# Attention with top-32 masking, then a gated MLP, on one core: the second exponential ahead of the score copies, normalisation in the same turn, and w3's products issued from a list

## The chip, the cores and the metric

The kernel runs on one core of a Trainium2 chip. The metric is the device time of one execution in microseconds (us), lower being better. The five engines are named as in the profile: PE (TensorE matmul, with PEld for its weight loads), DVE (VectorE), ACT (ScalarE), POOL (GpSimd) and SP (SyncE, which issues all DMAs here).

## What is computed

Batch 8, 8 heads, 576 positions, head dimension 64; all float32. Cut to what matters, the reference is:

```python
scores = np.matmul(q, k.transpose(0, 1, 3, 2)) / np.sqrt(D)
kth = np.partition(scores, -32, axis=-1)[..., -32:-31]
scores = np.where(scores >= kth, scores, -1e9)
attn = np.exp(scores - scores.max(-1, keepdims=True))
attn = attn / (attn.sum(-1, keepdims=True) + 1e-9)
x = np.matmul(attn, v)                # heads joined: 4608 tokens x 512
return ((x @ w1) * (x @ w2)) @ w3 @ w_out     # 512 -> 1024 -> 1024 -> 512
```

The kernel multiplies w3 with w_out once, at the start, and uses the product (wf) for all tokens.

## The kernel before, in words

**Slots and turns.** The attention is cut into 144 slots, 18 for each batch entry. A slot is 128 query rows of two heads, or, for every fifth of a head pair (t == 4), the last 64 rows of two head pairs. The main loop of `attn_moe` runs one turn per value of `p`, and works on four slots in it: scores of slot i = p+1 (PE), the search for the 32 largest of slot p (DVE), mask and exponentials of slot j = p-1 (ACT and POOL), and transposes, values and output of slot m = p-2 (PE, ACT, DVE). An engine runs its instructions in the order in which the code issues them (`InOrder`).

**Names.** `st` are the two PSUM tiles of a slot's scores, `s` their copy in SBUF. `w` is the search's working copy, `top` the 32 maxima, `edge` what bias the mask and the exponential need from them. `pab` holds a slot's weights: the mask (ACT, then a POOL subtraction `pab<-s,pab`), the exponential (ACT, with the row sums `sums`), and the normalisation (POOL, `pab<-pab,sums`), for which `enlarge` adds 1e-9 to the sums on POOL and `invert` takes their reciprocal on DVE. `tp` and `ro` are the transposes, `pts` and `pr` their copies (ACT), and `ro` then takes the values' product too; `xf` is the attention's output, as a high half (ACT) and a low half (DVE).

**PSUM.** Transposes and scores share one pool of two buffers (`ps_a`): in a turn tp, st and st take them in rotation, so that the next turn's tp waits until the first st has been copied by ACT and read by DVE's first two search instructions. `ro` has one buffer, which is free again when DVE has read it for the low half of xf. The third pool (three buffers) serves the MLP, the weights' decoding and w3's products.

**The MLP.** Every 18 turns a batch entry's MLP is queued as a list of 576 matmuls. `fill(SHARE[k])` issues 11, 11 and 10 of them at three places of each turn. Their results are taken by closures (`take_a`: ACT copy `asb`; `take_b`: DVE product `whole`, ACT cast `g`, POOL remainder `g`; `take_o`: ACT copy `osb` and a DMA), which `evict()` issues at the head of the next fill. Two thirds of the matmuls are ab (x times w1 and w2), one third eo (times wf).

**The start.** Weights arrive as 64-bit values and are decoded on the way (ACT twice, DVE twice, POOL once for each of 40 pieces: 8 of w_out, 16 of w3, 8 of w1, 8 of w2), in steps that `warm()` advances at five places of a turn; every second call starts another piece. A w3 piece issues its four products with w_out (`pf`) as soon as it is decoded, wherever that falls in the turn; when a tile pf is complete, ACT and DVE split it into wf.

Of the kernel before, what the change touches and what calls it, by code (L numbers as in the profile page):

```python
# [14 lines left out]
ALU = mybir.AluOpType  # L15
# [42 lines left out]
def attn_moe(ctx: ExitStack, tc: tile.TileContext, q, k, v, w1, w2, w3, w_out, out, flag, general):  # L58
# [12 lines left out]
    pe, act, dve, pool, sp = nc.tensor, nc.scalar, nc.vector, nc.gpsimd, nc.sync  # L71
# [26 lines left out]
    if not general:  # L98
        pe, act, dve, pool, sp = (InOrder(tc, e) for e in (pe, act, dve, pool, sp))
# [7 lines left out]
    def decode(z, dst=None):  # L107

        t = ps_m.tile([128, 512], F32, tag="mm", name="t")
        y = x_p.tile([128, 4 * HS], F32, tag="x", name="y")
        high = z[:, 1:1024:2]
        low = z[:, :1024].bitcast(U16)[:, 1:2048:4]
        u, r = y[:, :512].bitcast(I32), y[:, 512:1024].bitcast(I32)
        sign = z[:, :512].bitcast(I32)
        act.activation(t, high, AF.Copy, scale=2.0**-112)
        act.activation(r, low, AF.Copy, scale=2.0**-13)  # L120
        yield
        ti = t.bitcast(I32)
        dve.tensor_scalar(sign, ti, -(2**31), None, op0=ALU.bitwise_and)
        dve.scalar_tensor_tensor(u, ti, 3, sign, op0=ALU.logical_shift_left, op1=ALU.bitwise_or)
        yield
        dst = y[:, :512] if dst is None else dst
        pool.tensor_tensor(dst.bitcast(I32), u, r, op=ALU.add)
        yield
        yield
        return dst  # L130
# [10 lines left out]
    def load_wout(c, z):  # L141
        yield from decode(z, wo[:, c * 512 : (c + 1) * 512])

    fold = {}

    def load_w3(c, z):
        f, i = c // 2, c % 2
        y = yield from decode(z)
        if i == 0:
            fold[f] = ps_m.tile([128, 512], F32, tag="mm", name=f"pf{f}")  # L150
        for j in range(4 * i, 4 * i + 4):
            pe.matmul(
                fold[f], y[:, (j % 4) * 128 : (j % 4 + 1) * 128], wo[:, j * DM : (j + 1) * DM],
                start=(j == 0), stop=(j == NFC - 1),
            )
        if i == 1:
            cut = slice(f * DM, (f + 1) * DM)
            yield
            act.copy(wf[0][:, cut], fold[f])
            yield  # L160
            dve.tensor_tensor(wf[1][:, cut], fold[f], wf[0][:, cut].bitcast(F32), op=ALU.subtract)
# [37 lines left out]
    def new_s():  # L199
        return att_p.tile([128, 2, S], F32, tag="s", name="s", bufs=3)  # L200
# [5 lines left out]
    def behind(ins, first, why):  # L206
        tc.add_manual_dep(
            ins.ins, first.ins.name, mybir.DependencyInfo(mybir.DependencyClass.Sync, mybir.DependencyReason.DATA),
            reason=why,
        )  # L210

    def top32_steps(s, st, taken, slot):

        w = att_p.tile([128, 2, S], F32, tag="w", name="w", bufs=1)
        top = tops[slot % len(tops)]  # L220
        one, two, three = slice(0, NG), slice(NG, 2 * NG), slice(2 * NG, S)
        in_two, in_three = st[0][:, :, NG : 2 * NG], st[1][:, :, :NG]
        dve.tensor_tensor(w[:, :, three], s[:, :, one], in_two, op=ALU.max)
        yield dve.tensor_tensor(w[:, :, two], s[:, :, one], in_two, op=ALU.min)
        ins = dve.tensor_tensor(w[:, :, one], w[:, :, three], in_three, op=ALU.max)
        behind(ins, taken, "one engine at a time reads a bank of the scores")
        dve.tensor_tensor(w[:, :, three], w[:, :, three], in_three, op=ALU.min)
        yield
        for i in range(4):
            cut = slice(i * 8, (i + 1) * 8)  # L230
            for a in range(2):
                dve.max(top[:, a, cut], w[:, a, one] if i < 3 else w[:, a, :])
            if i < 3:
                for a in range(2):
                    dve.match_replace(w[:, a, one], top[:, a, cut], w[:, a, one], NEG)
                yield
# [7 lines left out]
    def compare(slot):  # L244
        top = tops[slot % len(tops)]
        pool.tensor_tensor(over[:, 2 * slot : 2 * slot + 2], top[:, :, 31], top[:, :, 23], op=ALU.subtract)
# [23 lines left out]
    def exps(edge, pab, sums, a):  # L270
        p = pab[:, a, :]
        act.activation(p, p, AF.Exp, bias=edge[:, a, 0:1], scale=SCALE, accum_out=sums[:, a : a + 1])

    def enlarge(sums):
        pool.tensor_scalar(sums, sums, 1e-9, None, op0=ALU.add)

    def invert(sums):
        dve.reciprocal(sums, sums)

    def normalise(pab, sums):  # L280
        for a in range(2):
            pool.tensor_scalar(pab[:, a, :], pab[:, a, :], sums[:, a : a + 1], 1.0, op0=ALU.mult, op1=ALU.mult)
# [40 lines left out]
    def take_high(to, ov):  # L323
        for x, cols, n in to:
            act.copy(x[:, 0, cols], ov[:, n])

    def take_low(to, ov):
        for x, cols, n in to:
            dve.tensor_tensor(x[:, 1, cols], ov[:, n], x[:, 0, cols].bitcast(F32), op=ALU.subtract)
# [69 lines left out]
    if general:  # L399
# [3 lines left out]
        with tc.For_i(0, B, 1) as b:  # L403
            seen = small.tile([1, 1], I32, tag="seen", name="seen", bufs=1)
            nc.sync.dma_start(seen, flag[ds(b + 1, 1), :])
            with tc.If(nc.values_load(seen, min_val=0, max_val=1) > 0):
                kv, xs = {}, {}
                for hps, t in SLOTS:
# [3 lines left out]
                    s, st = new_s(), scores([kv[hp] for hp in hps], t)  # L412
# [20 lines left out]
    kv, ss, sts, edges, pabs, xts, lows = {}, {}, {}, {}, {}, {}, {}  # L433
# [4 lines left out]
    def evict():  # L438
        while put_off:
            put_off.pop(0)()  # L440

    def fill(n):
        evict()
        while queue and n:
            if next(queue[0], "end") == "end":
                queue.pop(0)
            else:
                n -= 1
# [4 lines left out]
    def fetch_pair(u):  # L453
        if u < B * NHP:
            kv[u] = load_pair(u // NHP, u % NHP)

    waiting = list(startup)
    fetched, going, turns = [], [], []

    def prefetch(n):  # L460
        while waiting and len(fetched) < n:
            src, step = waiting.pop(0)
            fetched.append((fetch(src), step))

    def warm():

        if p < 0:
            return
        turns.append(p)
        if fetched and len(turns) % 2:  # L470
            z, step = fetched.pop(0)
            going.append(step(z))
        going[:] = [unit for unit in going if next(unit, "end") != "end"]
        prefetch(3)
# [4 lines left out]
    n_slots = len(slots)  # L479
    for p in range(-1, n_slots + 3):  # L480
        i, j, m = p + 1, p - 1, p - 2
        if i < n_slots and slots[i][1] == 3:
            fetch_pair(slots[i][0][0] + 2)
        finder = top32_steps(ss[p], *sts.pop(p), p) if 0 <= p < n_slots else iter(())
        next(finder, None)
        if 0 <= m < n_slots:
            enlarge(pabs[m][1])
            invert(pabs[m][1])
        if 0 <= j < n_slots:
            edges[j] = edges_of(j)  # L490
        if 0 <= m < n_slots:
            normalise(*pabs[m])
        next(finder, None)
        if m - 1 in lows:
            take_low(*lows.pop(m - 1))
            if m % NS == 0:
                b = m // NS - 1
                queue.append(moe_steps(b, [xts.pop(b * NHP + hp) for hp in range(NHP)], put_off.append))
        warm()
        if 0 <= j < n_slots:  # L500
            pabs[j] = new_weights()
            for a in range(2):
                mask(ss[j], edges[j], pabs[j][0], a)
            compare(j)
        fill(SHARE[0])
        next(finder, None)
        if 0 <= m < n_slots:
            tp, ro = turn(pabs[m][0])
            pts, pr = take_turned(tp, ro)
        warm()  # L510
        if 0 <= j < n_slots:
            exps(edges[j], *pabs[j], 0)
        fill(SHARE[1])
        next(finder, None)
        warm()
        if i < n_slots:
            st = scores(pairs_of(i), slots[i][1])
            ss[i] = new_s()
            take_scores(ss[i], st, 0)
        if 0 <= j < n_slots:  # L520
            exps(edges[j], *pabs[j], 1)
        if i < n_slots:
            sts[i] = st, take_scores(ss[i], st, 1)
        if 0 <= m < n_slots:
            us, t = slots[m]
            for u in us:
                if u not in xts:
                    xts[u] = new_x()
            ov = values([kv[u][2] for u in us], t, pts, pr, ro)
            lows[m] = places([xts[u] for u in us], t), ov  # L530
            take_high(*lows[m])
        next(finder, None)
        warm()
        fill(SHARE[2])
        for _ in finder:
            pass
        if 0 <= m < n_slots:
            del ss[m], pabs[m], edges[m]
        warm()
# [61 lines left out]
```

## Time and profile before

| | |
|---|---|
| median of 3 runs | 1324.32 us (1323.19 to 1325.38) |
| the profiled execution | 1324.6 us, span from its first to its last instruction 1322.8 us |
| busy: PE, DVE | 1225.7 us (93%), 1144.5 us (87%) |
| busy: ACT, POOL | 949.1 us (72%), 863.2 us (65%) |
| mean granted TensorE clock | 0.977 of full speed |

Shares over the whole span mix three stages: the start up to some 230 us, in which the weights are decoded beside the first 18 slots; the steady part, in which each turn carries its 32 MLP matmuls; and the last 93 us, in which only the last entry's MLP is left. So busy time is read by stage below. PE's matmuls are pipelined, so that a row's length is more than what it adds; what a group of matmuls costs is read from one start to the next.

### The profile page before, as it was taken

What the parts mean: (1) busy time and instruction counts of PE and PEld (TensorE: products, weight loads), DVE (VectorE), ACT (ScalarE), POOL (GpSimd) and SP (SyncE); (2) the same over time, 40 slices, a digit from 0 to 9 for tenths busy, and PEclk for the clock granted to TensorE, in tenths of its full rate; (3) what the DMA queues carried; (4) which work ended last, traced back from release to release, by engine and by line L of the source; (5) the groups of instructions that cost most, each with busy time, mean ns of one, the idle gap of its engine ahead of it and who ended that gap; (6) DMA issues with size and microseconds to landing.
All of it is one profiled execution on the core that took longest, in us unless ns stands there. A gap on an engine that the chain in (4) does not pass through costs nothing.

```text
span 1322.8 us, 30010 instructions
## 1 busy us (share of the span) xinstructions
PE 1225.7 (93%) x10513; PEld 1045.4 (79%) x10513; DVE 1144.5 (87%) x3980; ACT 949.1 (72%) x2025; POOL 863.2 (65%) x1201
## 2 busy tenths in 40 slices
PE   3688846999999999999999999999999999999996
PEld 1444424888888889888888888888988888888996
DVE  7989889999999999999999999999999999999100
ACT  5776687777777787777777777777777777777311
POOL 4767697776767676766667676767677676667210
PEclk9899877999999999999999999999999999999998
DMA  6343320001020201110010101010111001000000
GB/s 232 115 139 112 126 94 23 28 22 59 17 64 12 68 13 49 31 50 20 27 53 21 59 17 63 13 50 30 49 31 48 22 21 59 17 15 2 19 19 21
DMA packets 28981, 63.89 MB, mean 48 GB/s; under 512 B 3220, under 2 KB 11412, under 8 KB 28820
## 3 DMA queue, kind: packets, MB, share of 16 engines
q1 hardware_dynamic: 28820, 61.88, 14.4%
q8 instruction: 85, 1.39, 0.5%
q14 instruction: 76, 0.62, 0.2%
HBM read 52.43 MB, written 9.44 MB: 47 GB/s over the span
## 4 chain that ended last, share of the span: by engine, by line
PE 75%; POOL 10%; ACT 7%; issue 4%; DVE 3%; DMA 0%; SPq 0%; POOLq 0%; ACTq 0%; DVEq 0%
PE ab L49 26%; PE eo L49 16%; PE st L49 11%; PE ro L49 11%; PE tp L49 9%; POOL pab L49 5%; PE pf L49 3%; ACT pab L49 2%; ACT s L49 2%; POOL g L49 2%; DVE w L49 1%; POOL y L49 1%; DVE top L49 1%; ACT g L49 1%; ACT xf L49 1%
## 5 line engine op out<-in xcount | busy, mean ns | idle before, releaser
L49 DVE MAX8 top<-w 128x8 f32<-128x192 f32 (+1 forms) x1152 | 469.1, 451 | 0.0
L49 PE MATMUL ab<-xf,wh 128*128 128x288 f32 x2048 | 430.6, 300 | 0.0
L49 POOL TENSOR_TENSOR pab<-s,pab 128x576 f32<-128x576 f32 x288 | 404.6, 1429 | 4.7 <-ACT pab L49 4.7
L49 PEld LDWEIGHTS ab<-xf,wh 128*128 128x128 f32 x2048 | 331.3, 189 | 8.3 <-issue 7.4
L49 PE MATMUL ab<-xf,wl 128*128 128x288 f32 x1024 | 307.4, 300 | 0.0
L49 DVE MATCH_REPLACE8 w<-top,w 128x192 f32<-128x192 f32 x864 | 291.2, 347 | 0.0
L49 POOL TENSOR_SCALAR pab<-pab,sums 128x576 f32<-128x576 f32 x288 | 212.5, 753 | 78.4 <-DVE sums L49 57.9
L49 ACT COPY pts<-tp 128x1024 f32<-128x1024 f32 x144 | 146.2, 1015 | 152.7 <-PE tp L49 151.0
L49 ACT ACTIVATE pab<-s,edge 128x576 f32<-128x576 f32 x288 | 209.6, 782 | 54.6 <-POOL edge L49 52.4
L49 PE MATMUL eo<-g,wf 128*128 128x288 f32 x1536 | 228.4, 300 | 0.0
L49 ACT ACTIVATE pab<-pab,edge 128x576 f32<-128x576 f32 x288 | 225.2, 782 | 1.6 <-POOL pab L49 1.3
L49 PE MATMUL tp<-ident,pab 128*128 128x128 f32 x1152 | 166.1, 284 | 64.8 <-POOL pab L49 53.6
L49 ACT COPY s<-st 128x768 f32<-128x768 f32 (+1 forms) x288 | 181.9, 632 | 48.2 <-PE st L49 39.8
L49 PEld LDWEIGHTS eo<-g,wf 128*128 128x128 f32 x1536 | 208.1, 188 | 7.2 <-issue 7.2
L49 PEld LDWEIGHTS tp<-ident,pab 128*128 128x128 f32 x1152 | 134.6, 144 | 88.6 <-POOL pab L49 87.2
L49 PE MATMUL st<-kt,qt 64*128 64x192 f32 (+3 forms) x1280 | 188.8, 445 | 16.0 <-ACT pab L49 7.4
L49 PEld LDWEIGHTS ab<-xf,wl 128*128 128x128 f32 x1024 | 193.6, 189 | 4.8 <-issue 4.8
L49 POOL TENSOR_TENSOR g<-whole,g 128x288 fp32r<-128x288 f32 x128 | 103.0, 805 | 139.7 <-ACT g L49 139.7
L49 DVE TENSOR_TENSOR w<-s,st 128x384 f32<-128x384 f32 x288 | 146.7, 551 | 29.4 <-ACT s L49 18.3
L49 PEld LDWEIGHTS st<-kt,qt 64*128 64x128 f32 (+1 forms) x1280 | 100.2, 182 | 88.9 <-issue 34.8
L49 DVE TENSOR_TENSOR w<-w,st 128x384 f32<-128x384 f32 x288 | 157.7, 548 | 5.0
L49 PE MATMUL ro<-pts,vt 128*64 128x128 f32 (+1 forms) x2560 | 161.5, 269 | 0.0
(46 smaller groups left out, 1128.5 us busy)
## 6 DMA issues: line engine op xcount, KB each, us to landing
z<-in_w SPq DMA_DIRECT2D x32, 512.0 KB, 3.6
vt<-in_v SPq DMA_DIRECT2D x32, 352.0 KB, 3.5
kt<-in_k SPq DMA_DIRECT2D x32, 320.0 KB, 3.3
qt<-in_q SPq DMA_DIRECT2D x32, 288.0 KB, 2.9
out_t<-osb SPq DMA_DIRECT2D x64, 144.0 KB, 1.7
z<-in_wo SPq DMA_DIRECT2D x8, 512.0 KB, 5.0
flag<-missed SPq DMA_DIRECT2D x1, 0.0 KB
seen<-flag SPq DMA_DIRECT2D x1, 0.0 KB
```

The source lines that it names most:

```text
L49: ins = fn(*args, **kw)
```

## The change

In a turn, the first four search instructions now stand together; the second exponential follows the first, ahead of both score copies (before: copy, second exponential, copy). `enlarge`, `invert` and `normalise` work on slot j, behind its exponentials, in place of slot m at the head of the next turn: `enlarge` behind the cast of xf, the reciprocal on DVE behind the third search round and ahead of the last maxima, the normalisation on POOL behind it. w3's products go to a list, from which a turn takes up to 3 behind the masks, 1 behind the exponentials (between transposes and scores on PE) and 4 behind the values; a piece waits until its last product has been issued, and at most four pieces are under way.

```diff
+    fold, heavy = {}, []
+    def weigh(n):
+        while heavy and n:
+            heavy.pop(0)()
+            n -= 1
...
-        for j in range(4 * i, 4 * i + 4):
+        def product(j):
             pe.matmul(
...
+        heavy.extend((lambda j=j: product(j)) for j in range(4 * i, 4 * i + 4))
+        last = heavy[-1]
...
+        while last in heavy:
+            yield
...
-        yield dve.tensor_tensor(w[:, :, two], s[:, :, one], in_two, op=ALU.min)
+        dve.tensor_tensor(w[:, :, two], s[:, :, one], in_two, op=ALU.min)
...
-        if fetched and len(turns) % 2:
+        if fetched and len(turns) % 2 and len(going) < 4:
...
-        next(finder, None)
-        if 0 <= m < n_slots:
-            enlarge(pabs[m][1])
-            invert(pabs[m][1])
...
-        if 0 <= m < n_slots:
-            normalise(*pabs[m])
...
+        weigh(3)
         fill(SHARE[0])
...
             exps(edges[j], *pabs[j], 0)
+            exps(edges[j], *pabs[j], 1)
+        weigh(1)
         fill(SHARE[1])
...
             take_scores(ss[i], st, 0)
-        if 0 <= j < n_slots:
-            exps(edges[j], *pabs[j], 1)
-        if i < n_slots:
             sts[i] = st, take_scores(ss[i], st, 1)
...
             take_high(*lows[m])
+        if 0 <= j < n_slots:
+            enlarge(pabs[j][1])
         next(finder, None)
         warm()
+        if 0 <= j < n_slots:
+            invert(pabs[j][1])
+            normalise(*pabs[j])
+        weigh(4)
         fill(SHARE[2])
```

On POOL, in a turn of the steady part that carries two of the MLP's `g` and the turn behind it (pab<-pab,sums is the normalisation, pab<-s,pab the mask's subtraction), before:

```order
L49 TENSOR_TENSOR g<-whole,g 128x288 x2
L49 TENSOR_SCALAR sums<-sums 128x2
L49 TENSOR_TENSOR edge<-top_95,coef 128x4
L49 TENSOR_SCALAR pab<-pab,sums 128x576 x2
L49 TENSOR_TENSOR pab<-s,pab 128x576 x2
L49 TENSOR_TENSOR over<-top_95 128x2
L49 TENSOR_TENSOR g<-whole,g 128x288
L49 TENSOR_SCALAR sums<-sums 128x2
L49 TENSOR_TENSOR edge<-top_96,coef 128x4
```

and now:

```order
L49 TENSOR_TENSOR g<-whole,g 128x288
L49 TENSOR_SCALAR sums<-sums 128x2
L49 TENSOR_SCALAR pab<-pab,sums 128x576 x2
L49 TENSOR_TENSOR g<-whole,g 128x288
L49 TENSOR_TENSOR edge<-top_95,coef 128x4
L49 TENSOR_TENSOR pab<-s,pab 128x576 x2
L49 TENSOR_TENSOR over<-top_95 128x2
L49 TENSOR_TENSOR g<-whole,g 128x288
L49 TENSOR_SCALAR sums<-sums 128x2
L49 TENSOR_SCALAR pab<-pab,sums 128x576 x2
```

The normalisation and one g have moved from behind and ahead of the sums to the other side of the edge; the last g still stands ahead of the sums.

On DVE, the second of these turns (MAX of 128x8 from w are the search rounds, the last of them over the whole row), before:

```order
L49 TENSOR_TENSOR w<-s,st 128x2x192 x2
L49 RECIPROCAL sums<-sums 128x2
L49 TENSOR_TENSOR w<-w,st 128x2x192 x2
L49 TENSOR_TENSOR xf<-ro,xf 128x64 x2
L49 MAX top_96<-w 128x8 x2
L49 MATCH_REPLACE w<-top_96,w 128x192 x2
L49 TENSOR_TENSOR whole<-ab,asb 128x288
...
L49 MATCH_REPLACE w<-top_96,w 128x192 x2
L49 MAX top_96<-w 128x8 x2
L49 TENSOR_TENSOR w<-s,st 128x2x192 x2
L49 RECIPROCAL sums<-sums 128x2
```

and now:

```order
L49 TENSOR_TENSOR w<-s,st 128x2x192 x2
L49 TENSOR_TENSOR w<-w,st 128x2x192 x2
L49 TENSOR_TENSOR xf<-ro,xf 128x64 x2
L49 MAX top_96<-w 128x8 x2
L49 MATCH_REPLACE w<-top_96,w 128x192 x2
L49 TENSOR_TENSOR whole<-ab,asb 128x288
...
L49 MATCH_REPLACE w<-top_96,w 128x192 x2
L49 RECIPROCAL sums<-sums 128x2
L49 MAX top_96<-w 128x8 x2
L49 TENSOR_TENSOR w<-s,st 128x2x192 x2
```

The reciprocal has left the head of the turn for the place ahead of the last maxima.

On PE, the fourth slot's transposes at the start (pf are w3's products), before:

```order
L49 MATMUL tp<-ident,pab 128x128 x8
L49 MATMUL ro<-ident,pab 128x128
L49 MATMUL pf_585<-wo,y 128x512 x4
L49 MATMUL st<-kt,qt 128x384 x2
L49 MATMUL st<-kt,qt 128x192 x2
L49 MATMUL ro<-pts,vt 64x128 x8
L49 MATMUL ro<-pr,vt 64x128 x2
L49 MATMUL pf_585<-wo,y 128x512 x4
```

and now:

```order
L49 MATMUL tp<-ident,pab 128x128 x8
L49 MATMUL ro<-ident,pab 128x128
L49 MATMUL pf_585<-wo,y 128x512
L49 MATMUL st<-kt,qt 128x384 x2
L49 MATMUL st<-kt,qt 128x192 x2
L49 MATMUL ro<-pts,vt 64x128 x8
L49 MATMUL ro<-pr,vt 64x128 x2
L49 MATMUL pf_585<-wo,y 128x512 x7
```

Three of the four products between transposes and scores have moved behind the values.

## Rows read from the trace of the kernel before

**Rows 1.** Busy time by stage: stage, length, each engine's busy us (instructions), clock, DMA.

```profile
0.00:230.00 230.00, 151.54 (x875) 87.16 (x876) 200.03 (x606) 161.90 (x316) 159.93 (x197) 0.89 0.36 120
...
400.00:600.00 200.00, 198.62 (x1806) 175.90 (x1805) 189.21 (x680) 153.99 (x333) 137.90 (x198) 1.00 0.12 37
```

**Rows 2.** Waits from 250 to 1220 us: total us, times, longest.

```profile
PEld tp L49 <- POOL pab L49: 20.0, 54, 0.5
```

**Rows 3.** The chain that ended last, 376 to 400 us: start, us, what.

```profile
376.28 0.87 PE tp L49 x8
...
384.10 0.87 PE tp L49 x8
384.97 0.11 PE ro L49
...
389.92 0.81 POOL g L49
...
390.79 0.21 POOL sums L49
...
393.49 0.11 PE ro L49
```

**Rows 4.** Timeline of DVE, 384 to 400 us (start, us, instruction, idle before).

```profile
391.04 0.17 DVE L49 RECIPROCAL sums<-sums 128x2 f32<-128x2 f32 x1 [0.80 <-POOL sums L49]
391.12 1.15 DVE L49 TENSOR_TENSOR w<-w,st 128x384 f32<-128x384 f32 x2
...
396.26 1.42 DVE L49 MAX8 top<-w 128x8 f32<-128x576 f32 x2
397.79 1.02 DVE L49 TENSOR_TENSOR w<-s,st 128x384 f32<-128x384 f32 x2
...
399.84 0.28 DVE L49 TENSOR_TENSOR xf<-ro,xf 128x128 fp32r<-128x128 f32 x1
```

**Rows 5.** Timeline of PE, 704 to 719 us.

```profile
712.54 1.03 PE L49 MATMUL tp<-ident,pab 128*128 128x128 f32 x8
```

**Rows 6.** Timeline of ACT, 704 to 719 us.

```profile
705.84 1.02 ACT L49 COPY pts<-tp 128x1024 f32<-128x1024 f32 x1 [0.54 <-PE tp L49]
...
706.90 0.79 ACT L49 ACTIVATE pab<-pab,edge 128x576 f32<-128x576 f32 x1
...
707.67 0.43 ACT L49 CAST g<-whole 128x288 fp32r<-128x288 f32 x1
...
708.89 0.78 ACT L49 ACTIVATE pab<-pab,edge 128x576 f32<-128x576 f32 x1
...
713.67 1.01 ACT L49 COPY pts<-tp 128x1024 f32<-128x1024 f32 x1 [0.40 <-PE tp L49]
```

**Rows 7.** Timeline of POOL, 704 to 719 us.

```profile
708.18 0.80 POOL L49 TENSOR_TENSOR g<-whole,g 128x288 fp32r<-128x288 f32 x1 [0.22 <-ACT g L49]
709.86 0.21 POOL L49 TENSOR_SCALAR sums<-sums 128x2 f32<-128x2 f32 x1 [0.88 <-ACT pab L49]
```

**Rows 8.** What DVE waited for from 60 to 210 us: total us, times, longest.

```profile
DVE z L49 <- ACT y L49: 13.5, 11, 3.0
DVE wf L49 <- ACT wf L49: 3.5, 2, 2.5
```

**Rows 9.** Timeline of DVE, 56 to 80 us.

```profile
60.53 0.69 DVE L49 TENSOR_TENSOR wf<-pf,wf 128x512 fp32r<-128x512 f32 x1 [1.07 <-ACT wf L49]
...
74.50 0.69 DVE L49 TENSOR_SCALAR z<-t 128x512 int32<-128x512 int32 x1 [3.05 <-ACT y L49]
```

**Rows 10.** Timeline of DVE, 121 to 150 us.

```profile
135.68 0.69 DVE L49 TENSOR_TENSOR wf<-pf,wf 128x512 fp32r<-128x512 f32 x1 [2.48 <-ACT wf L49]
...
149.63 0.69 DVE L49 TENSOR_SCALAR z<-t 128x512 int32<-128x512 int32 x1 [3.05 <-ACT y L49]
```

**Rows 11.** Timeline of PE, 60 to 90 us.

```profile
65.11 5.26 PE L49 MATMUL pf<-wo,y 128*128 128x512 f32 x8
```

**Rows 12.** Timeline of ACT, 62 to 80 us.

```profile
71.26 0.80 ACT L49 COPY s<-st 128x768 f32<-128x768 f32 x1 [3.01 <-PE st L49]
```

More of the change, by code (lines that the diff above doesn't have):

```diff
@@ L142, in load_wout @@
         yield from decode(z, wo[:, c * 512 : (c + 1) * 512])
-    fold = {}
+    fold, heavy = {}, []
[3 more added lines that the diff above has]
+            n -= 1
     def load_w3(c, z):
@@ L155, in load_w3 @@
             )
+        heavy.extend((lambda j=j: product(j)) for j in range(4 * i, 4 * i + 4))
+        last = heavy[-1]
+        if general:
+            weigh(4)
+        while last in heavy:
+            yield
         if i == 1:
@@ L531, in attn_moe @@
             take_high(*lows[m])
+        if 0 <= j < n_slots:
+            enlarge(pabs[j][1])
         next(finder, None)
         warm()
+        if 0 <= j < n_slots:
+            invert(pabs[j][1])
+            normalise(*pabs[j])
+        weigh(4)
         fill(SHARE[2])
```

## The prediction

> **What bounds the kernel now.** I read busy time by stage first, because the shares of the whole span mix stages with different limits [rows 1]. From 400 to 600 us PE is busy 198.6 of 200 us and DVE 189.2: PE sets the pace and DVE is only 5% behind it. In the start (0 to 230 us) it is the other way round: DVE is busy 200.0 of 230 us, PE 151.5. So a gain in the steady part can only come from time in which PE stands still, and one in the start from time in which DVE does.
>
> Then I followed the chain that ended last. In an undisturbed steady turn it is PE alone: transposes start at 376.28 and again at 384.10, a pace of 7.82 us [rows 3]. The next turn is the kind that is disturbed. The chain leaves PE for ACT and POOL: MLP remainder g at 389.92, sums at 390.79, then the normalisation, and the ro transpose comes at 393.49, 8.52 us behind the last one (384.97). That is 0.70 us lost, about half ahead of the transposes and half inside them, as each head's normalisation arrives. The waits say how often: 54 weight loads of tp waited for POOL's pab between 250 and 1220 us, two in each disturbed turn, so 27 such turns [rows 2]. 27 x 0.70 = 18.9 us is all that the steady part can give. The last 93 us are MLP matmuls alone, and no edit touches them: 0.
>
> For the start I asked what DVE waited for. From 60 to 210 us it waited 13.5 us for decoded halves from ACT and 3.5 us for ACT's part of wf [rows 8].
>
> **The change part by part.** Nothing is added or removed in number: the same matmuls, copies, POOL and DVE instructions and the same DMAs, issued by SP in the same order. What counts is who stands behind whom.
>
> *Normalising a turn earlier.* The wait of tp for the normalisation goes: in the new order the two normalisations (1.5 us) follow the reciprocal at the end of a turn, while tp of that slot comes after the next fill. That returns the 0.70 us in each of the 27 turns, if nothing else is late.
>
> *What is late next.* The reciprocal now stands on DVE between the third search round and the last maxima, and it needs the sums, which need both exponentials. Behind the waiting reciprocal stand the last maxima and the next turn's four search instructions. PE waits for these: tp needs the st buffer that the first two of them read, and ro needs its one buffer, which the xf instruction behind all four frees. I walk this loop from one tp (time 0) to the next:
>
> - the copy pts starts at 1.13 (712.54 to 713.67) [rows 5, 6];
> - the first exponential 1.06 later (705.84 to 706.90), the second 0.77 after it (706.90 to 707.67, one exponential) [rows 6]: 2.96;
> - the sums 0.97 behind the start of the second exponential (708.89 to 709.86) [rows 6, 7]: 3.93;
> - the reciprocal 0.25 later (390.79 to 391.04) [rows 3, 4]: 4.18; the maxima 0.08 after it, the next search instruction 1.53 after those (396.26 to 397.79) [rows 4]: 5.79.
>
> The first two search instructions last 1.02 and xf starts some 1.97 behind them (2.05 less the reciprocal's 0.08) and lasts 0.28 [rows 4]; with 0.08 us for the signal (707.67 + 0.43 to 708.18) [rows 6, 7], tp may start at 6.89 and ro at 8.12. PE wants them at 7.82 and 8.69 (0.87 later). So an ordinary turn has 0.57 us to spare. The second exponential's move costs nothing either: the first score copy now starts at 2.96 + 0.77 = 3.73 and lasts 0.80 [rows 12], so it is done at 4.53, with 1.26 us of cover before DVE wants it at 5.79; without that cover its lateness would be DVE's.
>
> In two turns of nine it is different. These are the second turns of the order shown for POOL: an MLP cast g stands on ACT behind both exponentials, and POOL's g ahead of the sums. Before, these g's delayed nothing that PE wanted. Now the loop is longer: cast at 2.96 + 0.77 = 3.73, POOL's g 0.51 later (707.67 to 708.18) [rows 6, 7], the sums 0.87 behind it (389.92 to 390.79) [rows 3], reciprocal at 5.36, next search at 6.97. tp may start at 8.07, 0.25 late, and ro at 9.30, 0.61 late. So about 0.61 us is lost, once for each 0.70 that is lost now, one turn later. 27 x (0.70 - 0.61) = 2.4 us gained. Both ends: 18.9 us gained, if that reciprocal is not late; below, the rival that it is late everywhere.
>
> First what the row shows on which this hangs: DVE stood idle for 0.80 us ahead of the reciprocal at 391.04, and the search instruction behind it, whose inputs were there, started only at 391.12 [rows 4]. [...]
>
> *w3's products.* Before, 4 products may stand between tp and st on PE (the row's 8 records are 4 products, two each): 5.26 us [rows 11]. Behind them waited st, its copy on ACT (3.01 us idle until 71.26) [rows 12], behind that copy ACT's next decoding, and for that DVE, 3.05 us at 74.50 [rows 9]. The same happens six turns later at 149.63, 3.05 us [rows 10]. Twice, at 60.53 and 135.68, DVE waited 1.07 and 2.48 us for wf, whose products ran late on PE [rows 9, 10]. Now one product at most stands there, a quarter of 5.26 us, and st needs tp's copy in that time anyway; the others run behind the values, where the next transposes have the fill's place to wait. I take these four waits as gone: 3.05 + 3.05 + 1.07 + 2.48 = 9.65 us, since DVE bounds the start. Both ends: 13.5 + 3.5 = 17.0 us, if all of these waits go [rows 8]; 0, if DVE's time is lost again at the reciprocal, which now stands behind POOL's decoding steps too. I come near the middle: in the start a turn of DVE carries one to three decoding steps more ahead of the reciprocal, so that DVE comes to it later than in a steady turn, and the one or two decoding steps that POOL has ahead of the sums are covered by that.
>
> The limit of four pieces under way I cost at nothing: a turn starts 2.5 pieces and can issue 8 products, where it needs 6.7.
>
> *Sum*, against the profiled execution's own 1324.6 us (span 1322.8, and 1.8 around it; the median of the runs shown is 1324.32, 0.3 lower): 1324.6 - 9.65 - 2.4 = 1312.5 us.
>
> **The rivals.** All times from 1324.6. Forecast: 1312.5.
>
> *The stall goes altogether.* If in the two turns of nine the reciprocal is no later than DVE reaches it, or the ro buffer is free sooner than I reckon, the steady part runs at 7.82 us throughout: 1324.6 - 9.65 - 18.9 = 1296. For it: DVE is only busy 189 of 200 us, and can catch up. Against it: the loop above exceeds the pace by 0.61 us, and its parts are all measured.
>
> *The start gives nothing.* If the reciprocal's wait replaces the waits for ACT: 1324.6 - 2.4 = 1322.2. For it: sums now have decoding steps on POOL ahead of them in most turns, and DVE in the start has little slack. Against it: the walk above.
>
> *Slower: the reciprocal is late in every turn with ab matmuls.* The price is paid if ACT or POOL are more than 0.57 us later at the sums than in the loop above, for instance because POOL's mask subtraction ends behind the first exponential. If the six of nine turns that carry ab were all as late as the two with g, four more in nine, 54 in all, would lose 0.61 us: 33 us, so 1312.5 + 33 = 1345.5. The point from which it decides is that 0.57. Against it: POOL has lost the normalisation ahead of the subtraction, so it starts sooner.
>
> **How the numbers follow.** Forecast 0.52, stall gone 0.20, start gives nothing 0.18, slower 0.10. The prediction is 1312.5; its own range, with 5 us of the start's waits and 0.1 us for each of the 27 turns either way (2.7 us), is 1305 to 1320. The range of 8 in 10 takes in the first two rivals: 1295 to 1323; it leaves out the slower one and the outer parts of the others. A change of 0.2% (2.6 us) is about what a measurement of this kernel can tell from none. Faster than that are the forecast, the gone stall and 0.07 of the rival without a start's gain; within it 0.08 of that rival; slower the remaining 0.03 and the slower rival's 0.10. So 0.79, 0.08 and 0.13.
>
> **What would show it.** tp should no longer wait for POOL's pab in the steady part. If I am right, DVE waits for the sums at the reciprocal by 0.5 us in ordinary turns and by over 1 us in two turns of nine, and there PE waits for DVE (tp for w, ro for xf) by about 0.6 us; undisturbed turns stay at 7.82. In the start, DVE's busy share from 60 to 210 us should rise, and the first ab matmul should come about 10 us sooner than now. The prediction is wrong if PE's turns show no gap at all (then 1296), or gaps in all turns with ab, or if the first ab matmul is not earlier.

## The result, and the profile after

The changed kernel takes 1304.92 us (median of 4 runs, 1303.69 to 1306.99) against 1323.76 us (1322.28 to 1325.38, 4 runs): a ratio of 0.9859, 95% interval 0.9841 to 0.9878. Forecast were 1312.5 us, range 1295 to 1323. The direction is right and the time lies in the range, but 7.6 us under the forecast. The profiled execution's span fell from 1322.8 to 1302.4 us, by 20.4 us.

To see where these come from, I split both spans at the first transposes of the first turn that has MLP matmuls. PE's timeline, before and then after (start, us, instruction, idle before):

```profile
231.77 1.38 PE L49 MATMUL tp<-ident,pab 128*128 128x128 f32 x8 [0.15 <-POOL pab L49]
```

```profile
214.00 1.06 PE L49 MATMUL tp<-ident,pab 128*128 128x128 f32 x8 [0.61 <-ACT pab L49]
```

The start is 17.8 us shorter (forecast: 9.65). What follows it went from 1322.8 - 231.8 = 1091.0 to 1302.4 - 214.0 = 1088.4 us: 2.6 us (forecast: 2.4).

**The steady part.** Busy time by stage, after (columns as in [rows 1]):

```profile
0.00:230.00 230.00, 165.31 (x1032) 101.41 (x1033) 215.79 (x664) 175.13 (x345) 172.71 (x216) 0.90 0.38 125
250.00:1200.00 950.00, 945.36 (x8607) 835.18 (x8607) 898.22 (x3217) 727.55 (x1590) 656.40 (x940) 1.00 0.11 35
```

and the waits from 250 to 1200 us, those of PE's loads and of DVE (total us, times, longest):

```profile
DVE sums L49 <- POOL sums L49: 32.3, 51, 0.9
...
PEld ro L49 <- DVE xf L49: 9.0, 27, 0.3
PEld tp L49 <- issue: 7.5, 27, 0.3
```

The row of [rows 2], tp (the transposes) waiting for POOL's pab, is gone. In its place ro waits 27 times for DVE's xf and tp 27 times ("issue": what releases its buffer isn't named): 9.0 / 27 + 7.5 / 27 = 0.61 us each time. The chain through one of these turns shows the whole loop (start, us, what):

```profile
373.69 0.89 PE tp L49 x8
...
374.65 1.02 ACT pts L49
...
375.83 1.51 ACT pab L49 x4
377.35 0.33 ACT g L49
...
377.75 0.80 POOL g L49
...
378.62 0.23 POOL sums L49
...
378.87 0.17 DVE sums L49
...
380.45 0.61 DVE w L49 x2
...
382.44 0.30 DVE xf L49
...
382.78 0.33 PE ro L49
```

This tp starts at 373.52 in the timeline. Behind it stand pts at 1.13, POOL's g at 4.23, the sums at 5.10, the reciprocal (the row "DVE sums") at 5.35, the next search instruction at 6.93, and ro at 9.26; the prediction's walk has 1.13, 4.24, 5.11, 5.36, 6.97 and 9.30. DVE's timeline shows it idle for 0.82 us ahead of that reciprocal:

```profile
378.87 0.17 DVE L49 RECIPROCAL sums<-sums 128x2 f32<-128x2 f32 x1 [0.82 <-POOL sums L49]
```

PE's next transposes stand at 381.62, 8.10 us on, and the ones behind at 389.81, 8.19 us on, instead of 7.82:

```profile
381.62 1.07 PE L49 MATMUL tp<-ident,pab 128*128 128x128 f32 x8
...
389.81 1.03 PE L49 MATMUL tp<-ident,pab 128*128 128x128 f32 x8
```

**The start.** DVE's waits from 60 to 210 us, after:

```profile
DVE z L49 <- ACT y L49: 1.9, 6, 0.5
DVE sums L49 <- POOL sums L49: 1.1, 2, 0.6
```

In [rows 8] the first of these was 13.5 us, with 3.5 us more for wf. Nearly all of it has gone, where I had taken four waits of 9.65 us. The waits at the reciprocal, 1.5 us before, are 1.1 us, so its new place cost DVE nothing more there. DVE is busy 215.8 of the first 230 us, before 200.0 [rows 1]. Up to the first of the transposes used above, its busy time is 201.8 us before and 200.1 us after: of the 17.8 us, 16.2 are idle time of DVE that went, and 1.6 are shorter busy time.

### The profile page after: what moved, and what is told of

The parts are those of the page before. It is cut to its first block, busy times and chain, and to the rows that moved or that the text cites. A ratio compares the mean times of both kernels' runs of the same rounds, so it can differ in the third digit from the quotient of the medians.

```text
span 1302.4 us, 30009 instructions
## 1 busy us (share of the span) xinstructions
PE 1222.0 (94%) x10513; PEld 1044.2 (80%) x10513; DVE 1144.1 (88%) x3980; ACT 942.3 (72%) x2025; POOL 863.4 (66%) x1201
## 4 chain that ended last, share of the span: by engine, by line
PE 67%; DVE 14%; ACT 10%; issue 4%; POOL 4%; DMA 0%; DVEq 0%; ACTq 0%; SPq 0%; POOLq 0%
PE ab L49 24%; PE eo L49 15%; PE ro L49 11%; PE st L49 9%; PE tp L49 8%; DVE w L49 5%; DVE top L49 5%; ACT pab L49 4%; ACT pts L49 3%; POOL g L49 2%; PE pf L49 1%; DVE y L49 1%; DVE z L49 1%; POOL pab L49 1%; DVE xf L49 1%
## 5 line engine op out<-in xcount | busy, mean ns | idle before, releaser
L49 ACT ACTIVATE pab<-pab,edge 128x576 f32<-128x576 f32 x288 | 221.9, 778 | 0.9 <-POOL pab L49 0.7
L49 PE MATMUL tp<-ident,pab 128*128 128x128 f32 x1152 | 155.3, 279 | 42.6 <-DVE w L49 28.5
L49 ACT COPY s<-st 128x768 f32<-128x768 f32 (+1 forms) x288 | 170.0, 648 | 4.3 <-PE st L49 4.3
```

The lines of the kernel that those rows point to most:

```text
L49: ins = fn(*args, **kw)
```

## The experiments

All were timed beside the kernel before (1324.94 us for the first four, 1323.69 for the last four, 7 runs each). "First tp" is the start of the transposes used above, from each trace; "rest" is the span less that.

| kernel | median us | ratio to before, 95% | first tp | rest |
|---|---|---|---|---|
| before | | | 231.77 | 1091.0 |
| the change | 1304.92 | 0.9859 (0.9841 to 0.9878) | 214.00 | 1088.4 |
| the list alone | 1312.33 | 0.9910 (0.9893 to 0.9928) | 219.62 | 1091.8 |
| the order alone | 1310.87 | 0.9902 (0.9884 to 0.9920) | 220.26 | 1088.5 |
| sums first | 1290.39 | 0.9746 (0.9729 to 0.9764) | 217.21 | 1071.2 |
| reciprocal last | 1310.25 | 0.9898 (0.9881 to 0.9916) | 217.67 | 1089.9 |
| copy first | 1388.51 | 1.0482 (1.0465 to 1.0500) | 218.55 | 1168.9 |
| four between | 1313.78 | 0.9922 (0.9905 to 0.9938) | 222.78 | 1088.9 |
| sums first, later | 1288.43 | 0.9724 (0.9707 to 0.9742) | 216.20 | 1071.7 |
| no limit | 1306.96 | 0.9869 (0.9852 to 0.9885) | 216.22 | 1088.5 |

### One part alone: the list

The kernel before, with w3's products on the list and the limit of four pieces; search, exponentials and normalisation stay as before.

```diff
+        heavy.extend((lambda j=j: product(j)) for j in range(4 * i, 4 * i + 4))
...
+        weigh(3)
         fill(SHARE[0])
...
+        weigh(1)
         fill(SHARE[1])
...
+        weigh(4)
         fill(SHARE[2])
```

> The kernel before with w3's list alone (3, 1 and 4 products at the three places, at most four pieces under way); exponentials and normalisation stand as before. Theory 1 (the start's 17.8 us come from the products that no longer stand between transposes and scores): the first transposes of the first MLP turn come 10 to 18 us sooner than before (231.8 us), the steady turns keep their 0.70 us stalls, so some 1306 to 1314 us against 1323.8 before. Theory 2 (they come from normalising a turn earlier, so that the transposes no longer wait for POOL): the list alone gives under 5 us, 1319 us or more.

Measured: 1312.33 us. The start is 12.2 us shorter, as by theory 1, the rest as before (54 waits for the normalisation still there). DVE's waits from 60 to 210 us:

```profile
DVE z L49 <- ACT y L49: 4.7, 9, 0.9
DVE sums L49 <- POOL sums L49: 1.5, 2, 1.2
```

### The other part alone: the order

The change without list and limit; the products are issued as soon as a piece is decoded.

```diff
-        heavy.extend((lambda j=j: product(j)) for j in range(4 * i, 4 * i + 4))
+        for j in range(4 * i, 4 * i + 4):
+            pe.matmul(
...
-        weigh(3)
-        weigh(1)
-        weigh(4)
```

> The changed kernel without the list: w3's four products are issued at once where their piece is decoded, as before; exponentials and normalisation stand as in the change. Theory 1: the start gains under 8 us, the steady part 2 to 3 us, so 1313 to 1321 us. Theory 2: the start gains 13 us or more, so 1309 us or less.

Measured: 1310.87 us. The rest is as in the changed kernel, as it must be. But the start is 11.5 us shorter too, with all four products still between transposes and scores: more than theory 1 had, less than theory 2. I had costed the order at nothing there. One thing that it changes is a wait that no group ahead of the prediction shows. The waits of PE's loads from 60 to 210 us, before:

```profile
PEld tp L49 <- POOL pab L49: 43.4, 15, 7.9
```

and with the order alone:

```profile
PEld tp L49 <- POOL edge L49: 19.4, 4, 7.1
PEld tp L49 <- POOL pab L49: 10.3, 3, 4.4
```

With the rows named "issue" and POOL's y, all of tp's waits there sum to 44.7 us before and 38.5 us with the order alone. So only a part of them goes, and these sums don't say how much of the 11.5 us it gives. One turn shows what the change does.

At the place of [rows 11], PE's timeline before reads

```profile
63.13 1.97 PE L49 MATMUL tp<-ident,pab 128*128 128x128 f32 x8 [3.69 <-POOL pab L49]
...
65.11 5.26 PE L49 MATMUL pf<-wo,y 128*128 128x512 f32 x8
70.30 1.24 PE L49 MATMUL st<-kt,qt 64*128 64x384 f32 x8
```

and with the order alone

```profile
61.16 1.06 PE L49 MATMUL tp<-ident,pab 128*128 128x128 f32 x8 [2.60 <-DVE w L49]
...
62.49 3.60 PE L49 MATMUL pf<-wo,y 128*128 128x512 f32 x8
66.02 1.24 PE L49 MATMUL st<-kt,qt 64*128 64x384 f32 x8
```

Before, the transposes had waited 3.69 us for the normalisation ahead of those products. Now they come when DVE has read the scores, the same four products take 3.60 instead of 5.26 us (see the last section), and st stands 4.86 us behind the start of tp instead of 7.17. In this turn, then, the waits of DVE that I had put down to the products alone had both delays ahead of them. With the order alone DVE's waits from 60 to 210 us are:

```profile
DVE z L49 <- ACT y L49: 7.5, 9, 1.8
DVE sums L49 <- POOL sums L49: 1.1, 2, 0.7
```

The order holds three moves (search instructions together, second exponential, normalisation); which of them gives how much of the 11.5 us wasn't run apart. With the list, the two kernels below that undo the exponential's move or put off the normalisation start some 4.6 and 3.7 us later than the change; 2 to 3 us of that are no more than executions differ by (the four runs of the change lie 3.3 us apart, and the first tp of two kernels whose first 18 turns stand in the same order 2.2 us, last section).

### The products between again, with the list

```diff
-        weigh(3)
         fill(SHARE[0])
...
-        weigh(1)
+        weigh(4)
         fill(SHARE[1])
```

> The changed kernel with the list kept, but up to four of w3's products again between the transposes and the scores (none behind the masks). Theory of the prediction (the four products between tp and st hold up the score copy, ACT's decoding behind it and DVE behind that): two waits of DVE of about 3 us and part of those for wf come back in the start, the first MLP turn comes 6 to 10 us later than in the changed kernel: 1311 to 1315. Rival (what the start lost was the order of sums and normalisation as much as the place of the products; with the order changed, ACT and DVE have room): the start is less than 3 us longer, 1304 to 1308. The steady part has no such products and stays as it is by both.

Measured: 1313.78 us, the start 8.8 us longer than in the changed kernel, as the theory said. So the products' place counts even with the new order. DVE's waits:

```profile
DVE z L49 <- ACT y L49: 8.6, 9, 2.4
DVE wf L49 <- ACT wf L49: 1.2, 1, 1.2
DVE sums L49 <- POOL sums L49: 1.1, 2, 0.6
```

Over these kernels one number follows the other. DVE's waits in this stretch (all rows of the view) sum to 18.7 us before (13.5 + 3.5 + 1.5 + 0.2), 10.9 here, 8.6 with the order alone, 6.2 with the list alone and 3.0 with both. Against before that is 7.8, 10.1, 12.5 and 15.7 us less, and the starts are 9.0, 11.5, 12.2 and 17.8 us shorter. DVE's busy time up to the first tp is nearly the same in all five, 200.1 to 201.8 us, so the start is this and DVE's idle time. Either part alone removes most of the waits, and so their gains, 12.2 and 11.5, don't add up.

### The limit

```diff
-        if fetched and len(turns) % 2 and len(going) < 4:
+        if fetched and len(turns) % 2:
```

> The changed kernel without the limit of four pieces under way. The prediction costed the limit at nothing, as a turn starts 2.5 pieces and can issue 8 products where it needs 6.7: no difference, 1302 to 1308. Rival (the limit holds pieces back in the start, so that weights come later than they could): 2 to 6 us faster; or (the limit keeps a piece's products from being late) 2 to 6 us slower.

Measured: 1306.96 us (1306.15 to 1307.79) against the changed kernel's 1303.69 to 1306.99. The medians differ by 2.0 us, the edge of the slower rival, and the ranges overlap: not told from none. The profiled execution's start is 2.2 us longer; its fourth slot's turn took 15.01 instead of 12.13 us, with PE's clock granted at 0.50 from 62 to 68 us instead of 1.00; that clock differed between executions (last section).

### Sums ahead of POOL's g

The changed kernel with the POOL instruction on the sums (0.21 us) issued right behind the two exponentials, ahead of the fill that issues the g.

```diff
             exps(edges[j], *pabs[j], 1)
+            enlarge(pabs[j][1])
         weigh(1)
         fill(SHARE[1])
...
-        if 0 <= j < n_slots:
-            enlarge(pabs[j][1])
         next(finder, None)
```

> The changed kernel with the small addition to the sums issued right behind the exponentials, so that on POOL it stands ahead of the MLP's g and not behind it. Theory (the loop over g, sums, reciprocal, last maxima and search holds PE up by 0.61 us in two turns of nine): with the sums some 1.2 us sooner in these turns the loop is below the pace of 7.82 us, both gaps go, 27 or 28 times 0.61 = 17 us: 1288 us, 1285 to 1292. Rival (DVE is too full in these turns, so the gaps come from its work and not from its wait at the reciprocal): the gaps stay, or half of them, 1296 to 1305 us.

Measured: 1290.39 us, 14.5 us less than the changed kernel. The rest is 17.2 us shorter; 27 x 0.61 is 16.5. POOL's timeline in the turn that answers to the chain above (its tp starts at 374.34):

```profile
378.26 0.21 POOL L49 TENSOR_SCALAR sums<-sums 128x2 f32<-128x2 f32 x1 [1.01 <-ACT pab L49]
378.57 0.80 POOL L49 TENSOR_TENSOR g<-whole,g 128x288 fp32r<-128x288 f32 x1
```

DVE's and PE's:

```profile
378.78 0.15 DVE L49 RECIPROCAL sums<-sums 128x2 f32<-128x2 f32 x1
```

```profile
382.15 1.04 PE L49 MATMUL tp<-ident,pab 128*128 128x128 f32 x8
...
389.97 1.04 PE L49 MATMUL tp<-ident,pab 128*128 128x128 f32 x8
```

The sums stand at 3.92 us behind tp instead of 5.10, the reciprocal no longer waits, and the pace is 7.81 and 7.82 us through both turns. Busy time of the stage:

```profile
250.00:1200.00 950.00, 950.00 (x8753) 851.40 (x8752) 902.66 (x3238) 741.18 (x1611) 663.82 (x953) 1.00 0.11 35
```

By this view PE has no gap left, and its turns from 241 us on take 7.77 to 7.93 us, but for the last two of the attention (6.7 us). DVE still waits at the reciprocal in one turn of three, mostly by 0.4 to 0.5 us; no turn is longer for it. This kernel beats both.

### Sums first, only where the MLP runs

Its start was 3.2 us longer than the changed kernel's. To see whether the sums' place does that, the first 18 turns keep the change's place.

```diff
+        early = p >= NS
+        if early and 0 <= j < n_slots:
+            enlarge(pabs[j][1])
...
-        if 0 <= j < n_slots:
+        if not early and 0 <= j < n_slots:
             enlarge(pabs[j][1])
```

> The small addition to the sums is issued behind the two exponentials, as in the kernel with sums first, but only from the turn on in which a batch entry's MLP can run; in the first 18 turns it stays where the change has it. Theory (in the steady part POOL's g ahead of the sums costs the 17 us; in the start the sums at that place make POOL's decoding steps wait for ACT, 3 us): the steady part as in the kernel with sums first, the start as in the changed kernel: 1390 - 103 = about 1287 us, 1285 to 1289. Rival (the 3 us of the start depend on something else, such as how the turns fall against the decoding): 1289 to 1292, no different from the kernel with sums first.

("1390 - 103" there is a slip of writing for 1290 - 3.) Measured: 1288.43 us (1287.06 to 1289.68), in the theory's range but only 0.6 us below the rival's; its interval overlaps that of sums first. Two of its four runs take 1287.1 to 1287.2 us, as the theory had it, and two, the profiled one among them, 1289.7 us, as the rival had it. In its first 18 turns the instructions stand in the changed kernel's order, and the profiled execution still came to the first tp 2.2 us later. So 2.2 of the 3.2 us can come without the sums' place. What differs in that execution is in the last section; the one profiled with sums first has the same two turns at 13.77 us each. All four runs with sums first take 1290.0 to 1290.6 us, so whether the sums' place plays a part stays open.

### The reciprocal behind the last maxima

```diff
-        if 0 <= j < n_slots:
-            invert(pabs[j][1])
-            normalise(*pabs[j])
...
         for _ in finder:
             pass
+        if 0 <= j < n_slots:
+            invert(pabs[j][1])
+            normalise(*pabs[j])
```

> The changed kernel with reciprocal and normalisation issued behind the last maxima. Theory: the maxima no longer queue behind a reciprocal that waits, so the next turn's search starts some 1.4 us sooner in the two turns of nine and the gaps go: 1288 to 1293 us; the normalisation then ends about 7.1 us behind the transposes' start, still ahead of the next transposes at 7.82. Rival (the normalisation is then late for the transposes, as before the change): PE waits for POOL's pab again, 1300 us or more.

Measured: 1310.25 us, as the rival had it; rest 1089.9, no better than the change. Waits from 250 to 1200 us:

```profile
DVE whole L49 <- ACT asb L49: 36.6, 54, 1.3
...
PEld tp L49 <- POOL pab L49: 8.5, 28, 0.4
...
DVE sums L49 <- POOL sums L49: 5.1, 27, 0.2
```

DVE's wait at the reciprocal fell from 32.3 to 5.1 us, but the wait of tp for the normalisation came back, and DVE now waits for asb. The wait moved; it didn't go.

### The second exponential back between the score copies

```diff
             exps(edges[j], *pabs[j], 0)
-            exps(edges[j], *pabs[j], 1)
...
             take_scores(ss[i], st, 0)
+        if 0 <= j < n_slots:
+            exps(edges[j], *pabs[j], 1)
+        if i < n_slots:
             sts[i] = st, take_scores(ss[i], st, 1)
```

> The changed kernel with the second exponential back between the two score copies; the sums, the reciprocal and the normalisation stay where the change put them. Theory (the loop from pts to the reciprocal sets the pace, and the exponential's move is what makes the loop fit into a turn): a score copy of 0.80 us enters the loop, so that sums come at 4.7 instead of 3.9 us and ro may start at 8.9 instead of 8.1 us behind tp, where PE wants it at 8.7: some 0.2 us lost in each of about 115 ordinary turns with MLP matmuls and some 0.8 us more in each of the 27 late turns, about 27 + 21 us: near 1353 us, 1335 to 1375. PE's turns are all above 7.82 us. Rival (DVE, which is only about 90% busy, catches up, or the copy falls where ACT was idle anyway): within 10 us of the changed kernel, 1300 to 1315.

Measured: 1388.51 us, 5% slower than before and above the expected 1335 to 1375. From 250 to 1190 us every turn takes 8.5 to 9.0 us. ACT's timeline of a turn without g, whose tp starts at 373.78:

```profile
376.00 0.79 ACT L49 ACTIVATE pab<-pab,edge 128x576 f32<-128x576 f32 x1
...
377.62 0.80 ACT L49 COPY s<-st 128x768 f32<-128x768 f32 x1 [0.73 <-PE st L49]
378.31 0.78 ACT L49 ACTIVATE pab<-pab,edge 128x576 f32<-128x576 f32 x1
```

DVE's:

```profile
379.52 0.17 DVE L49 RECIPROCAL sums<-sums 128x2 f32<-128x2 f32 x1 [1.11 <-POOL sums L49]
```

The copy not only lasts 0.80 us, it also waits 0.73 us for st, which the expectation had left out; in the chain st stands behind ro, and ro behind DVE's xf. The reciprocal stands at 5.74 us behind tp and DVE idles 1.11 us there; from 250 to 1200 us it idles there in all 110 turns, 99.9 us together. So the loop sets PE's pace. The exponential's move is thus what lets the normalisation come a turn earlier, and the slower rival's mechanism is real in this kernel, whose rest is 80 us longer.

## Why the prediction was right, and where it was off

**The removed stall and what replaced it** (2.4 us): right, to within some 0.04 us at each instruction of the loop, in the number of places (27) and in the loss (0.61 us). That POOL's g ahead of the sums causes it is shown by moving the sums: the rival "the stall goes altogether" did not happen in the change, and its 18.9 us are there to be had with one instruction more.

**What that hangs on.** In the chain DVE idles 0.82 us ahead of the reciprocal, and the search resumes only behind it: the last search instruction ahead of it ends at 378.05, the reciprocal starts at 378.87 and the maxima at 378.95. The copy-first kernel shows the same, where DVE idles there in every turn from 250 to 1200 us, by 0.91 us on average.

**DVE's waits at the reciprocal**: wrong in the details. I expected some 0.5 us in ordinary turns and over 1 us in the late ones. There were 0.66 to 0.88 us in the late ones and 0.46 us in 23 others, 51 waits in all, so that most ordinary turns had none: there DVE, with its own work in the turn, comes to the reciprocal later than the sums. PE's time hung only on the late ones.

**The start** (9.65 us): the term that was mis-sized; it measured 17.8. The step that failed is "I take these four waits as gone", with the order of the normalisation costed at nothing in the start. The order alone gave 11.5 us with the products where they were. I looked at what DVE waited for and stopped one engine short: tp's 43.4 us of waits for the normalisation stood ahead of the same scores, copies and decodings. That the order counts is shown; that it does so through tp's waits is read from the one turn above, and how much of the 11.5 us goes that way stays open. With both parts most of the small waits went as well, so the upper bound, 17.0 us, was the better value. That the total still lay in the range of 1295 to 1323 is owed to the room in it for the rivals; the forecast's own range, 1305 to 1320, ended 0.1 us above it. Of the 2 us between the 15.7 us of DVE's waits that went and the 17.8 of the start, 1.6 are DVE's shorter busy time, whose cause stays open; the start differs by as much between executions (2.2 us, last section). "The start gives nothing" was refuted: the waits at the reciprocal there were 1.1 us, and 1.5 before.

**The second exponential's move and the limit at nothing**: the limit within what can be told (medians 2.0 us apart). The exponential's move cost nothing, and undoing it costs 84 us; that was in the walk as 0.77 us of cover, but its weight was not.

**The slower rival**: didn't happen. The turns without g have no gap.

## What to carry to other kernels

Where a small instruction at the end of a chain over several engines stands in order on a busy engine, walk the loop from one iteration's start to the next with the trace's times; the loop's excess over the pace is the loss, and the instruction that another engine queues ahead of the small one is the first thing to move. Where two edits each shorten a chain of waits that ends on the bounding engine, price them together by that engine's total wait, not apart, and follow each of its waits back over more than one engine. When a wait has been removed, try whether one instruction placed elsewhere returns the rest: here 0.21 us of POOL work in another place gave 14.5 us.

## What the runs showed of the hardware

PE's clock was granted at 1.00 in one execution and at 0.51 to 0.64 in another in which PE's instructions stand in the same order. In the fourth slot's turn, the changed kernel and the one with sums first only later have the same order; the waits differ by half a microsecond. PE's timeline, changed kernel:

```profile
59.73 1.06 PE L49 MATMUL tp<-ident,pab 128*128 128x128 f32 x8 [1.01 <-DVE w L49]
...
62.31 1.10 PE L49 MATMUL pf<-wo,y 128*128 128x512 f32 x2 [1.09 <-DVE y L49]
63.34 1.24 PE L49 MATMUL st<-kt,qt 64*128 64x384 f32 x8
```

and the other:

```profile
59.61 1.06 PE L49 MATMUL tp<-ident,pab 128*128 128x128 f32 x8 [1.54 <-DVE w L49]
...
62.19 1.68 PE L49 MATMUL pf<-wo,y 128*128 128x512 f32 x2 [1.08 <-DVE y L49]
63.80 2.29 PE L49 MATMUL st<-kt,qt 64*128 64x384 f32 x8
```

Its stretch from 62 to 66 us (the figure ahead of the last two is the granted clock):

```profile
62.00:64.00 2.00, 1.81 (x4) 0.50 (x6) 2.00 (x10) 2.00 (x5) 2.00 (x3) 0.64 0.47 109
64.00:66.00 2.00, 2.00 (x8) 0.98 (x8) 1.97 (x8) 1.67 (x5) 1.54 (x3) 0.51 0.39 154
```

In the changed kernel this clock is 1.00 in both slices. At 0.51 to 0.64 st takes 2.29 instead of 1.24 us, and the turn 13.77 instead of 12.13 us; the same happens six turns later (13.78 against 12.13, with st again at 2.29 against 1.24; mean clock from 120 to 150 us 0.94 against 1.00), behind waits of 1.02 and 1.09 us against 1.00 and 1.09 us. So these two turns are 3.3 us longer by the level that the clock takes, the second time behind waits that differ by 0.02 us; the first tp of the MLP turns comes 2.2 us later, and other turns of the start differ as well. The kernel without the limit has the second place's waits to the hundredth (1.02 and 1.09 us) and keeps 1.00 there, with st at 1.24 us. How the level is chosen there these runs don't show: PE stood idle 1.02 to 1.54 us at these places where the level fell, but in the changed kernel it stood idle 1.00 to 1.09 us there and its clock stayed at 1.00.

The 5.26 us of [rows 11] were that too: before, the clock was granted at 0.50 there, behind tp's wait of 3.69 us,

```profile
64.00:66.00 2.00, 2.00 (x9) 1.48 (x8) 1.97 (x9) 0.81 (x1) 2.00 (x2) 0.50 0.20 27
```

and with the order alone, at 1.00, the same four products take 3.60 us. So in this turn a wait for the normalisation came with two losses, the wait itself and the slower products behind it. That the wait brought the clock down is read from the order of the two, not shown by a run that changes it alone; with the order alone PE stood idle 2.60 us ahead of tp there and its clock stayed at 1.00.
